# A feed-forward projection by seven block products instead of eight, with streamed weights and outputs summed in SBUF

## The chip, the cores and the metric

The kernel runs on one core of a Trainium2 chip. The metric is the device time of one execution in microseconds. Before the change three runs gave 747.5, 747.75 and 747.91 us, median 747.75. The profiled execution took 747.88 us; its span, from the first to the last recorded work, is 746.0 us.

The core has engines with a queue each: TensorE (PE) multiplies matrices into PSUM, an accumulator memory of eight banks of 128 x 512 floats; VectorE (DVE), ScalarE (ACT) and GpSimd (POOL) work element by element; SyncE (SP) issues the transfers between HBM and SBUF, the on-chip memory.

## The reference

Two branches share an input x of 2048 tokens by 640 features and are mixed by a gate g = sigmoid(x . gate_w):

```python
q, k, v = split(x @ wqkv)                 # 32 heads of 20
phi(a)  = concat(softmax(a @ w_phi), softmax(-(a @ w_phi)))   # per head
a = (phi(q) @ (phi(k)^T v)) / (phi(q) @ sum(phi(k)) + 1e-6) @ wo
h = silu(x @ w1)                          # w1: 640 x 1728
b = h @ w2                                # w2: 1728 x 640
out = g * a + (1 - g) * b
```

All is float32. The change concerns `h` and `b`, called the dense part.

## The kernel before, in words

Everything is computed transposed: features lie on the 128 partitions and tokens along the free axis. 640 features make NC = 5 chunks of 128. The 1728 hidden features make NF = 13 tiles of 128 and a remainder of 64, which counts as tile number 13 (`NF`). The 2048 tokens make NB = 4 blocks of 512.

Float32 accuracy comes from splitting each operand into a high part (rounded to the matmul's input format) and a low part (the difference): `split` (line 124) has ScalarE write the high part and VectorE or GpSimd the low part. A product is then three passes, `PASSES`: high by high, high by low, low by high. For the remainder tile both parts of the weight lie side by side in one stationary operand.

The work has three stages.

1. Keys, values and their state (lines 286 to 706). For 16 token tiles TensorE projects keys and values (`kv_proj`), VectorE and ScalarE make the softmax features (`k_spikes`, `k_sums`), and TensorE sums the state (`kv_acc`). At the end of it the first four hidden tiles of token block 0 are already computed (`h_first`, line 550) as filling, and the state goes to HBM (`kv_out`, then the store to `kv_d` at line 707).
2. The dense part. For each block `dense(b)` (line 936) holds five PSUM banks `acc`, one per output chunk. `h_parts` (line 524) computes one hidden tile in a further bank: 3 passes x 5 chunks = 15 matmuls with 512 tokens each. ScalarE applies silu in place and writes the high part of `u`; VectorE writes the low part. `out_acc` (line 719) then adds that tile's contribution to the five accumulators: 5 x 3 = 15 matmuls. The remainder tile takes 10 and 10. The order of tiles is `ORDERS`; the outputs lag by two tiles. After the last tile `acc_out` multiplies an accumulator by the gate row and stores it to `fb_d` in HBM. All split weights stay in SBUF for the four blocks; `load_f` (line 261) loads and splits them one after the other, nine of them during stage 1 (`NPRE`).
3. In block 3 `last_dense` (line 985) puts other work between the tiles: the fused query weights (`fused`, line 241), the state's layout (`make_kvw`), the split of `wo`, and the query features of the last four token tiles (`q_tile`, `q_rest`). After the dense part (line 1121) the loop `step` does the rest of the queries, the attention's outputs, the product with `wo` and the sum with the rows of `fb_d` (`n_mm`, `w_mm`, `w_add`).

`inorder(...)` fixes an engine's order to the written one. Where it does not name an engine, SyncE above all, a scheduler at build time chooses the order. `raw` gives four buffers for data just loaded; a load waits until the split of the data four loads earlier has been done.

Of the kernel before, what the change touches and what calls it, by code (L numbers as in the profile page):

```python
# [16 lines left out]
P = 128  # L17
# [26 lines left out]
ORDER = (*range(NF - 4), NF, *range(NF - 4, NF))  # L44
END = (0, 4, 5, 6, 7, 8, 9, 1, 2, 3, NF, 10, 11, 12)
ORDERS = (ORDER, ORDER, ORDER, END)
# [16 lines left out]
NEARLY = 3  # L63
PASSES = ((0, 0), (0, 1), (1, 0))
# [3 lines left out]
def mix_kernel(ctx: ExitStack, tc: tile.TileContext, xT, wqT, wkc, wkr, wv, bd, bdc, cst, wo, w1, w1r, w2, out):  # L68
# [61 lines left out]
    PE, DVE, ACT, POOL = E.PE, E.DVE, E.Activation, E.Pool  # L130
# [126 lines left out]
    seq = [(w, f) for f in range(NF) for w in (1, 2)]  # L257
    W = {}
    held = {}

    def load_f(n):
        w, f = seq[n]
        k = n - NPRE
        if 0 <= k < 10:
            if k % 5 == 0:
                held[k // 5] = big(f"f{k // 5}")
            t = held[k // 5][:, k % 5]
        else:
            t = wslot(f"w{w}_{f}", F32R).rearrange("p (s d) -> p s d", s=2) if n < NPRE else fp.tile([P, 2, D], F32R, name=f"w{w}_{f}")
        r = raw(f"wr{w}_{f}")  # L270
        src = w1[f] if w == 1 else w2[f * P : (f + 1) * P, :]
        nc.sync.dma_start(r[:, :D], src)
        split(t[:, 0, :], t[:, 1, :], r[:, :D], "pool" if n < NPRE else "dve")
        W[w, f] = t
# [249 lines left out]
    def h_parts(b, f):  # L524

        ph = bank(f"ph{b}_{f}")
        xt = X["f", b]
        u = slot(f"u{b}_{f}", fu, "u", 3)
        hs = ph
        if f == NF:  # L530
            hs = ur = fu.tile([P, 512], F32, tag="ur", name=f"ur{b}_{f}", bufs=2)
        if f < NF:
            todo = [(W[1, f][:, hw, c * P : (c + 1) * P], xt[c][:, hx, :]) for hw, hx in PASSES for c in range(NC)]
        else:
            todo = [(W1R[:, c, :], xt[c][:, hx, :]) for hx in range(2) for c in range(NC)]
        for n, (lhs, rhs) in enumerate(todo):
            nc.tensor.matmul(ph, lhs, rhs, start=(n == 0), stop=(n == len(todo) - 1))  # L537
        yield u
        if f < NF:
            nc.scalar.activation(hs, ph, AF.Silu)  # L540
            split(u[:, 0, :], u[:, 1, :], hs)
        else:
            nc.scalar.copy(ur[:FR], ph[FR:])
            nc.vector.tensor_tensor(ur[:FR], ph[:FR], ur[:FR], op=ALU.add)
            nc.scalar.activation(ur[:FR], ur[:FR], AF.Silu)
            nc.scalar.copy(u[:FR, 0, :], ur[:FR])
            nc.vector.tensor_tensor(u[FR:, 0, :], ur[:FR], u[:FR, 0, :].bitcast(F32), op=ALU.subtract)
        yield

    def h_first(f, chunks):  # L550

        for c in chunks:
            for hw, hx in PASSES:
                nc.tensor.matmul(  # L554
                    kvp[f % 2],
                    W[1, f][:, hw, c * P : (c + 1) * P],
                    X["f", 0][c][:, hx, :],
                    start=(c == 0 and hw == 0 and hx == 0),
                    stop=(c == NC - 1 and hw == 1),
                )  # L560

    def u_silu(f):
        us0[f] = slot(f"u0_{f}", fu, "u", 3), fu.tile([P, 512], F32, tag="ur", name=f"ur0_{f}", bufs=2)
        last["silu"] = nc.scalar.activation(us0[f][1], kvp[f % 2], AF.Silu)

    def u_hi(f):
        u, ur = us0[f]
        nc.scalar.copy(u[:, 0, :], ur)

    def u_lo(f):  # L570
        u, ur = us0[f]
        nc.vector.tensor_tensor(u[:, 1, :], ur, u[:, 0, :].bitcast(F32), op=ALU.subtract)
        us0[f] = u

    def h_tile(b, f):
        part = h_parts(b, f)
        u = next(part)
        next(part)
        return u
# [23 lines left out]
    us0 = {}  # L603
    phs, eks = {}, {}
    X["f", 0] = []
    xf0 = x_loads("f", 0, X["f", 0])
    with inorder(ACT, DVE, POOL):
# [41 lines left out]
        rw = raw("wr2_3")  # L649
        w23 = wslot("w2_3", F32R).rearrange("p (s d) -> p s d", s=2)  # L650
        nc.sync.dma_start(rw[:, :D], w2[3 * P : 4 * P, :])
        W[2, 3] = w23
        with inorder(PE):
# [4 lines left out]
            kv_rest(t - 2, phs[t - 2])  # L658
            v_part(t, 0, 0)
# [18 lines left out]
            nc.scalar.copy(w23[:, 0, :], rw[:, :D])  # L678
# [10 lines left out]
            nc.gpsimd.tensor_tensor(w23[:, 1, :], rw[:, :D], w23[:, 0, :].bitcast(F32), op=ALU.subtract)  # L689
# [11 lines left out]
            kv_out()  # L701
            u_lo(2)
            nc.vector.tensor_scalar_add(g1, g1, 1.0)
            nc.vector.reciprocal(g, g1)
            nc.vector.tensor_scalar(g1, g, -1.0, 1.0, op0=ALU.mult, op1=ALU.add)
            u_silu(3)
    nc.sync.dma_start(kv_d[: KF + 1], kvo[1])
    u_hi(3)
    u_lo(3)
# [6 lines left out]
    def bank(name):  # L716
        return ps.tile([P, 512], F32, tag="bank", name=name, bufs=8)

    def out_acc(order, f, u, acc, m):
        ds = slice(m * P, (m + 1) * P)  # L720
        if f < NF:
            todo = [(W[2, f][:, hw, ds], u[:, hu, :]) for hw, hu in PASSES]
        else:
            todo = [(W2R[:, k, ds], u[:, 0, :]) for k in range(2)]
        for n, (lhs, rhs) in enumerate(todo):
            nc.tensor.matmul(  # L726
                acc[m], lhs, rhs, start=(f == order[0] and n == 0), stop=(f == order[-1] and n == len(todo) - 1)
            )

    with tc.issue_after(last["silu"].ins):  # L730
        for n in range(NPRE, len(seq)):
            load_f(n)
    r = raw("w1rr")
    W1R = fp.tile([P, NC, P], F32R, name="w1_r")
    rv = r[:, : NC * FR].rearrange("p (c f) -> p c f", f=FR)
    nc.sync.dma_start(r[:, : NC * FR], w1r)
    split(W1R[:, :, :FR], W1R[:, :, FR:], rv)
    r = raw("w2rr")
    W2R = fp.tile([P, 2, D], F32R, name="w2_r")
    for k in range(2):  # L740
        nc.sync.dma_start(r[k * FR : (k + 1) * FR, :D], w2[NF * P :, :])
    nc.scalar.copy(W2R[:, 0, :], r[:, :D])
    nc.vector.memset(W2R[FR:, 1, :].bitcast(F32), 0.0)
    nc.vector.tensor_tensor(W2R[:FR, 1, :], r[:FR, :D], W2R[:FR, 0, :].bitcast(F32), op=ALU.subtract)

    wor_raw = {}
# [5 lines left out]
    def wo_split(c):  # L752
        r = wor_raw.pop(c)
        split(WO[:, c, 0], WO[:, c, 1], r[:, :D])

# [14 lines left out]
    def q_proj(t):  # L770
        if t // 4 == NB - 1:
            parts = [bank(f"pq{t}_{j}")[:, None, :HALF] for j in range(2)]
# [163 lines left out]
    def dense(b):  # L936

        order = ORDERS[b]
        acc = [bank(f"acc{b}_{m}") for m in range(NC)]
        us = {} if b else us0  # L940

        def add(n):
            for m in range(NC):
                out_acc(order, order[n], us[order[n]], acc, m)

        def acc_mm(m):
            for f in order[-3:]:
                out_acc(order, f, us[f], acc, m)

        def acc_out(m):  # L950
            o = fp.tile([P, 512], F32, tag="o", name=f"o{b}_{m}", bufs=3)
            nc.vector.tensor_tensor(o, acc[m], gates[b], op=ALU.mult)
            nc.sync.dma_start(fb_d[m, :, b * 512 : (b + 1) * 512], o)

        return order, us, add, acc_mm, acc_out

    gates = {}

    def load_gates(b):
        if b == 0:  # L960
            pg = bank("pg")
            nc.tensor.transpose(pg[:NT, :P], g1, ident)
            gT = fs.tile([P, 8 * H], F32, tag="sm", name="gT", bufs=3)[:NT, :P]
            nc.scalar.copy(gT, pg[:NT, :P])
            nc.sync.dma_start(g_d, gT)
        gates[b] = fp.tile([P, 512], F32, tag="G1", name=f"G1_{b}", bufs=1)
        nc.sync.dma_start(gates[b], g_d.rearrange("t p -> (t p)")[b * 512 : (b + 1) * 512].partition_broadcast(P))

    for b in range(NB - 1):
        load_x("f", b + 1)  # L970
        order, us, add, acc_mm, acc_out = dense(b)
        for n, f in enumerate(order):
            if f not in us:
                us[f] = h_tile(b, f)
            if n == 4:
                load_gates(b)
            if 1 < n < NF:
                add(n - 2)
        for m in range(NC):
            acc_mm(m)  # L980
            acc_out(m)

    order, us, add, acc_mm, acc_out = dense(NB - 1)
# [405 lines left out]
```

## Time and profile before

| | |
|---|---|
| median of three runs | 747.75 us |
| profiled execution | 747.88 us |
| its span | 746.0 us |
| TensorE busy | 741.4 us, 4177 matmuls |
| VectorE, ScalarE, GpSimd busy | 347.3, 264.1, 255.3 us |
| transfers | 50.30 MB, 67 GB/s over the span |
| dense part on TensorE | 186.9 to 573.2 us |

A row of a group reads: line, engine, operation, output <- input by the program's names, shape, count, then busy time in us, mean duration of one in ns, and the idle time of its engine just before, with what ended it. A row of the timeline reads: start, duration, engine, line, operation. A row of the chain in order of time reads: start, duration, engine, output tile, line, count. The slices cut the span in 40 equal parts of 18.65 us; each digit is the busy share in tenths. PE's weight loads have rows of their own (PEld) and lie beside the matmuls. SPq is SyncE's queue of transfers.

### The profile page before, as it was taken

What the parts mean: (1) busy time and instruction counts of PE and PEld (TensorE: products, weight loads), DVE (VectorE), ACT (ScalarE), POOL (GpSimd) and SP (SyncE); (2) the same over time, 40 slices, a digit from 0 to 9 for tenths busy, and PEclk for the clock granted to TensorE, in tenths of its full rate; (3) what the DMA queues carried; (4) which work ended last, traced back from release to release, by engine and by line L of the source; (5) the groups of instructions that cost most, each with busy time, mean ns of one, the idle gap of its engine ahead of it and who ended that gap; (6) DMA issues with size and microseconds to landing.
All of it is one profiled execution on the core that took longest, in us unless ns stands there. A gap on an engine that the chain in (4) does not pass through costs nothing.

```text
span 746.0 us, 10458 instructions
## 1 busy us (share of the span) xinstructions
PE 741.4 (99%) x4177; PEld 648.0 (87%) x4177; DVE 347.3 (47%) x619; ACT 264.1 (35%) x477; POOL 255.3 (34%) x158
## 2 busy tenths in 40 slices
PE   9999999999999999999999999999999999999998
PEld 8899998888888888888888888888898899999988
DVE  5677666676651220112200122123566776867652
ACT  5444443346542311123111221123553544345230
POOL 2488777767100000000000000000174578686540
PEclk9999999999999999999999999999999999999999
DMA  7111111103650130001300013022102231221222
GB/s 262 53 54 54 54 54 54 60 34 97 199 193 1 50 106 1 1 0 53 107 0 1 0 42 121 36 77 73 39 29 104 74 104 52 86 78 57 72 86 78
DMA packets 35304, 50.30 MB, mean 67 GB/s; under 512 B 3546, under 2 KB 22890, under 8 KB 35255
## 3 DMA queue, kind: packets, MB, share of 16 engines
q1 hardware_dynamic: 35255, 49.63, 20.2%
q8 instruction: 33, 0.54, 0.3%
q14 instruction: 16, 0.13, 0.1%
HBM read 38.51 MB, written 11.11 MB: 67 GB/s over the span
## 4 chain that ended last, share of the span: by engine, by line
PE 99%; DVE 0%; ACT 0%; issue 0%
PE acc L726 25%; PE ph L537 23%; PE kvp L489 16%; PE pa L1182 10%; PE pq L448 10%; PE pn L1140 3%; PE pT L1007 2%; PE kv L459 2%; PE kvp L554 2%; PE kvp L344 1%; PE kvq L344 1%; PE pwk L332 1%; PE pwq L239 1%; PE warm L313 1%; PE kvp L470 0%; PE pkvt L916 0%
## 5 line engine op out<-in xcount | busy, mean ns | idle before, releaser
L127 DVE TENSOR_TENSOR u<-ph,u 128x512 fp32r<-128x512 f32 x48 | 33.2, 692 | 186.5 <-ACT u L125 186.5
L726 PE MATMUL acc<-u,w 128*128 128x512 f32 x480 | 113.6, 390 | 0.0
L909 POOL MEMSET kvw<- 120x40 f32 x1 | 0.1, 131 | 309.8 <-PE ph L537 309.8
L726 PEld LDWEIGHTS acc<-u,w 128*128 128x128 f32 x480 | 89.7, 188 | 18.6
L537 PE MATMUL ph<-xf,w 128*128 128x512 f32 x420 | 99.3, 389 | 0.0
L540 ACT ACTIVATE ph<-ph 128x512 f32<-128x512 f32 x48 | 27.9, 582 | 190.7 <-PE ph L537 190.6
L537 PEld LDWEIGHTS ph<-xf,w 128*128 128x128 f32 x420 | 78.7, 188 | 16.2
L489 PE MATMUL kvp<-wh,xa 128*128 128x480 f32 (+2 forms) x420 | 92.1, 355 | 0.0
L489 PEld LDWEIGHTS kvp<-wh,xa 128*128 128x128 f32 x420 | 71.9, 188 | 8.2
L1182 PE MATMUL pa<-oT,wo 128*128 128x256 f32 x600 | 77.0, 281 | 0.0
L1182 PEld LDWEIGHTS pa<-oT,wo 128*128 128x128 f32 x600 | 73.8, 188 | 0.8 <-DVE oT L1161 0.8
L824 POOL TENSOR_TENSOR ez<-eq,zbc 128x1280 f32<-128x1280 f32 x16 | 47.0, 2937 | 79.9 <-ACT eq L807 55.9
L726 PE MATMUL acc<-u,f 128*128 128x512 f32 x300 | 71.6, 390 | 0.0
L537 PE MATMUL ph<-xf,f 128*128 128x512 f32 x300 | 71.3, 389 | 0.0
L537 PEld LDWEIGHTS ph<-xf,f 128*128 128x128 f32 x300 | 56.3, 188 | 11.7
L726 PEld LDWEIGHTS acc<-u,f 128*128 128x128 f32 x300 | 56.1, 188 | 11.5
L127 POOL TENSOR_TENSOR ph<-ek,ph 128x1280 fp32r<-128x1280 f32 x16 | 47.5, 2966 | 25.8 <-ACT ph L125 24.4
L448 PE MATMUL pq<-wq,xb 128*128 128x320 f32 x360 | 55.9, 312 | 0.0
L448 PEld LDWEIGHTS pq<-wq,xb 128*128 128x128 f32 x360 | 52.9, 188 | 2.0 <-DVE oT L1161 1.6
L489 PE MATMUL kvp<-wl,xa 128*128 128x480 f32 (+2 forms) x210 | 47.2, 354 | 0.0
L807 ACT ACTIVATE eq<-eq 128x1280 f32<-128x1280 f32 x16 | 20.4, 1276 | 66.4 <-DVE eq L439 66.4
L517 POOL TENSOR_TENSOR ek<-ek,st 128x1280 f32<-128x1280 f32 x16 | 37.9, 2369 | 9.2 <-ACT v L304 6.1
(158 smaller groups left out, 1058.6 us busy)
## 6 DMA issues: line engine op xcount, KB each, us to landing
wr<-w SPq DMA_DIRECT2D x26, 320.0 KB, 4.0
xrf<-xT SPq DMA_DIRECT2D x20, 256.0 KB, 3.6
fb_d<-o SPq DMA_DIRECT2D x20, 256.0 KB, 2.4
y<-fb_d SPq DMA_DIRECT2D x16, 256.0 KB, 2.8
out<-y SPq DMA_DIRECT2D x16, 256.0 KB, 2.3
xra<-xT SPq DMA_DIRECT2D x14, 256.0 KB, 3.1
xrb<-xT SPq DMA_DIRECT2D x12, 256.0 KB, 2.7
wvr<-wv SPq DMA_DIRECT2D x5, 327.0 KB, 5.0
```

Of the source, the lines that this page charges most:

```text
L127: eng.tensor_tensor(lo, src, hi.bitcast(F32), op=ALU.subtract)
L344: nc.tensor.matmul(kv_cols(t, lo, hi), x_of(t)[c][:, hx, :], WKV[hw][:, c, w_cols(lo, hi)], start=(opens and hx == 0 and hw == 0), stop=(c ...
L448: nc.tensor.matmul(dst, xt[c][:, hx, :], w[:, c, hw, lo : lo + n], start=first, stop=(hx == 1 and c == NC - 1))
L489: nc.tensor.matmul(kv_cols(t, lo, hi), xt[c][:, hx, :], WKV[hw][:, c, w_cols(lo, hi)], start=(n == 0), stop=(n == 3 * NC - 1), skip_group_ ...
L517: nc.gpsimd.tensor_tensor(groups(e), groups(e), spread(st[:, 1, :]), op=ALU.mult)
L537: nc.tensor.matmul(ph, lhs, rhs, start=(n == 0), stop=(n == len(todo) - 1))
L540: nc.scalar.activation(hs, ph, AF.Silu)
L726: nc.tensor.matmul(acc[m], lhs, rhs, start=(f == order[0] and n == 0), stop=(f == order[-1] and n == len(todo) - 1))
L807: nc.scalar.activation(Q[t]["e"], Q[t]["e"], AF.Exp)
L824: nc.gpsimd.tensor_tensor(ez, Q[t]["e"], zbc, op=ALU.mult)
L1140: nc.tensor.matmul(pns[u, gp][side * CT : side * CT + lhs.shape[-1], a, :], lhs, f[:w, k * 256 : (k + 1) * 256], start=True, stop=True,)
L1182: nc.tensor.matmul(pa[:, a, :], WO[:, c, hw, ds] if c < NG else WOR[:, ds], o[:, ho, c, :] if c < NG else o[:GW, ho, c, :], start=(k == 0) ...
```

## The change

Hidden tiles are taken in pairs (f, g) = (2p, 2p + 1), and token blocks in two halves of two blocks. For four of the five input chunks a pair's 2 x 2 block matrix product (two tiles by two chunk pairs, times two chunk pairs by two blocks) is formed by seven block products instead of eight. They need four sums of weight blocks and four sums of x blocks; the results are combined by additions. The fifth chunk is multiplied directly. Tiles 12, 10, 11 and the remainder (`SINGLE`) of the first half and tile 12 and the remainder (`REG`) of the second are computed as before. So the first half has five pairs, the second six, of which the last (tiles 10 and 11) comes at the end.

- `pair_mm` yields between its eight groups of matmuls. Products that share a term are accumulated on one another in bank `a`, and read in between. `finish` applies silu in SBUF and splits.
- `out_items` gives the second projection for one pair, block and output chunk as a PSUM group of 6 matmuls (11 for four single tiles). VectorE adds it to `acc`, which is now in SBUF; the first group of a half is copied by ScalarE. At the end of a half GpSimd multiplies by the gate.
- PSUM is divided: two banks `a`, two `b`, four `o`.
- `pair_time` runs one pair's products with the previous pair's outputs between them (`PT`, `PTS`: how many after each), and spreads the preparation (`prep`) over the same places.
- `pair_weights` forms the weight sums and all splits of a pair (sums and low parts on GpSimd, high parts on ScalarE) and stores them to HBM (`w_d`), `w2_loads` the same for the second weight (`w2_d`); in the second half `pair_weights_again` and `w2_again` load the finished parts.
- The x sums are formed by `x_sum` and `x_part` into `XT`, for the first half at the start of the dense part, for the second half during pairs 5 and 6 (`half_sums`). The raw x of the first half for this lies in `acc[1]` and in two `w2` buffers.
- Three chunks of x for block 1 are loaded and split already at the end of stage 1 (`x1_hi`, `x1_lo`). The four early tiles are now 12, 10, 11 and the remainder.
- The end of the dense part is a written order of named pieces, `TAIL`. Query projections there use the `a` banks.
- The build reserves a smaller scratch for transfers (`dynamic_dma_scratch_size=1024`).

The core of the diff:

```diff
-NPRE = 9
+SINGLE = (12, 10, 11, NF)
+REG = (12, NF)
+NPAIR = 6
+PRE = ((1, 12), (1, 10), (1, 11), (1, NF), (2, 12), (2, 10), (2, 11), (2, NF), (1, 0))
...
+            xs1.extend(x1_hi(c) for c in range(3))
             h_first(3, (0,))
             kv_rest(t, phs[t], True)
             kv_acc(t, phs[t])
             h_first(3, range(1, NC))
+            x1_lo(xs1[0])
+            x1_lo(xs1[1])
             kv_out()
+            x1_lo(xs1[2], nc.vector)
...
+    def bank(name, tag="b"):
+        return ps.tile([P, 512], F32, tag=tag, name=name, bufs=4 if tag == "o" else 2)
...
+    def x_sum(i, r, eng=nc.gpsimd):
+        n, a, b = {1: (0, 1, 0), 3: (1, 3, 1), 2: (3, 3, 0), 4: (2, 2, 3)}[i]
+        eng.tensor_tensor(r[n], r[a], r[b], op=ALU.subtract)
+
+    def x_part(i, cc, r):
+        t, d = XT[i, cc], r[{1: 0, 3: 1, 2: 3, 4: 2}[i]]
+        nc.scalar.copy(t[:, 0, :], d)
+        nc.vector.tensor_tensor(t[:, 1, :], d, t[:, 0, :].bitcast(F32), op=ALU.subtract)
...
+    def pair_weights(n):
...
+        for dst, a, b, op in (
+            (a22, a21, a22, ALU.add),
+            (a21, a11, a21, ALU.subtract),
+            (a11, a22, a11, ALU.subtract),
+            (a12, a12, a11, ALU.subtract),
+        ):
+            nc.gpsimd.tensor_tensor(dst, a, b, op=op)
+            yield
+        for t, d in ((wb[:, :, 384:], a22), (wc[:, :, :256], a11), (wc[:, :, 256:], a21), (wd, a12)):
+            nc.scalar.copy(t[:, 0, :], d)
+            nc.gpsimd.tensor_tensor(t[:, 1, :], d, t[:, 0, :].bitcast(F32), op=ALU.subtract)
+            yield
+        WP[n][:] = wf, wb, wc, wd
+        if n < NPAIR - 1:
+            for k, t in enumerate(WP[n]):
+                nc.sync.dma_start(w_d[n][k], t.bitcast(F32))
...
+    def w2_loads(*tiles):
+        for f in tiles:
+            r = w_raw(2, f)
+            yield
+            t = w_tile(2, f, fp)
+            w_hi(2, f, t, r)
+            w_lo(2, f, t, r)
+            if f in w2_d and not kept.get(f):
+                nc.sync.dma_start(w2_d[f], t.bitcast(F32))
+                kept[f] = True
+            yield
...
+        def finish(fj, v):
+            u = U[fj] = u_tile(f"u{n}_{fj[0]}_{fj[1]}")
+            nc.scalar.activation(v, v, AF.Silu)
+            nc.scalar.copy(u[:, 0, :], v)
+            nc.vector.tensor_tensor(u[:, 1, :], v, u[:, 0, :].bitcast(F32), op=ALU.subtract)
+
+        a = bank(f"a{n}", "a")
+        mm(a, wf, 0, x0[:2], True, True)
+        yield
+        v1 = v_tile(f"v1_{n}")
+        nc.scalar.copy(v1, a)
+        yield
+        b = bank(f"b{n}")
+        mm(b, wf, 256, x0[2:4], True, False)
+        mm(b, wf, 512, x0[4:], False, True)
+        yield
+        yield
+        mm(a, ws[1], 384, t(1), False, True)
+        yield
+        v5 = v_tile(f"v5_{n}")
+        nc.vector.tensor_tensor(v5, v1, a, op=ALU.subtract)
+        nc.vector.tensor_tensor(v1, v1, b, op=ALU.add)
+        finish((f, 0), v1)
+        yield
+        d = bank(f"d{n}")
+        mm(d, ws[1], 0, t(4), True, False)
+        mm(d, ws[1], 256, x0[4:], False, True)
+        yield
+        yield
+        mm(a, ws[2], 0, t(2), False, True)
+        yield
+        v6 = v_tile(f"v6_{n}")
+        nc.scalar.copy(v6, a)
+        yield
+        c = bank(f"c{n}")
+        mm(c, ws[3], 0, x1[2:4], True, False)
+        mm(c, wf, 512, x1[4:], False, True)
+        yield
+        nc.vector.tensor_tensor(v6, v6, c, op=ALU.add)
+        finish((f, 1), v6)
+        yield
+        mm(a, ws[2], 256, t(3), False, False)
+        yield
+        nc.vector.tensor_tensor(v5, v5, a, op=ALU.add)
+        nc.vector.tensor_tensor(v5, v5, d, op=ALU.add)
+        finish((g, 0), v5)
+        yield
+        mm(a, ws[1], 256, x1[4:], False, True)
+        yield
+        finish((g, 1), a)
+        yield
...
+                for n, (lhs, rhs) in enumerate(todo):
+                    nc.tensor.matmul(o, lhs, rhs, start=(n == 0), stop=(n == len(todo) - 1))
+                yield
+                if start:
+                    nc.scalar.copy(acc[j][m], o)
+                else:
+                    nc.vector.tensor_tensor(acc[j][m], acc[j][m], o, op=ALU.add)
...
+    PT = (1, 1, 1, 1, 1, 1, 3, 1)
+    PTS = {0: (1, 0, 1, 0, 1, 2), NPAIR - 1: (3, 1, 1, 0, 1, 1, 2, 1), 2 * NPAIR - 2: (1, 1, 1, 1, 1, 0, 0, 0)}
...
+        first = pair_mm(0, 0)
+        twice(first)
+        next(first)
+        prep = thunks(pair_weights(0), 12) + prep
+        slots = 7
+        for f in SINGLE[:2]:
+            twice(h_tile(0, 1, f))
+            emit(prep, 0, slots)
+            slots -= 1
+        make_gates()
+        d2 = out_items(0, SINGLE, (0,), start=True)
+        for k in range(NC):
+            twice(d2)
+            emit(prep, 0, slots)
+            slots -= 1
+        for f in SINGLE[2:]:
+            twice(h_tile(0, 1, f))
+            emit(prep, 0, slots)
+            slots -= 1
...
+            if n == NPAIR - 2:
+                prep = merged(prep, half_sums())
+                load_gates(0)
...
+        for name in TAIL.split():
+            ops.pop(name)()
```

More of the change, by code (lines that the diff above doesn't have):

```diff
@@ L714, in mix_kernel @@
     ps = opened("psf", space=PSUM, reuse_waits="tile")
[L716 to L741, printed above, removed]
@@ L934, in mix_kernel @@
     es = {}
[L936 to L955, printed above, removed]
@@ L969, in mix_kernel @@
[L969 to L983, printed above, removed]
-    def last_dense(n, *extra):
-        part = h_parts(NB - 1, order[n])
-        us[order[n]] = next(part)
-        for w in extra:
-            next(w)
-        next(part)
-        if 1 < n < NF:
-            add(n - 2)
-        for w in extra:
-            next(w)
+    gates = {}
```

553 lines of the change are left out of this document (381 added, 172 removed).

## The prediction

> **What bounds the kernel now.** I read the engine totals first, then the slices, then the chain that ended last.
>
> ```profile
> PE 741.4 (99%) x4177; PEld 648.0 (87%) x4177; DVE 347.3 (47%) x619; ACT 264.1 (35%) x477; POOL 255.3 (34%) x158
> PE   9999999999999999999999999999999999999998
> DVE  5677666676651220112200122123566776867652
> POOL 2488777767100000000000000000174578686540
> GB/s 262 53 54 54 54 54 54 60 34 97 199 193 1 50 106 1 1 0 53 107 0 1 0 42 121 36 77 73 39 29 104 74 104 52 86 78 57 72 86 78
> PE 99%; DVE 0%; ACT 0%; issue 0%
> ```
>
> TensorE is busy in every slice and is 99% of the chain. Slices 11 to 28 are the dense part: VectorE has 0 to 2 tenths there and GpSimd nothing. So time goes away only with matmuls, and the other engines have room for what replaces them. The chain in order of time gives the price of a 512-column matmul:
>
> ```profile
> 372.90 3.40 PE ph L537 x15
> 376.31 3.40 PE acc L726 x15
> 410.31 3.40 PE acc L726 x15
> 413.70 2.27 PE ph L537 x10
> ```
>
> 15 matmuls take 3.40 us, 0.2267 us each. A hidden-tile product, one PSUM group of 15, and an output step, five groups of 3, have the same pitch: short groups and bank changes cost nothing. The table by stage (columns: stretch, length, then busy time and count of PE, PEld, DVE, ACT, POOL, then clock, DMA share, GB/s):
>
> ```profile
> 186.90:266.60 79.70, 79.70 (x354) 65.91 (x353) 31.94 (x47) 29.88 (x50) 2.08 (x3) 1.00 0.34 111
> 266.60:359.50 92.90, 92.90 (x411) 76.92 (x411) 16.77 (x25) 19.73 (x34) 0.00 (x0) 1.00 0.10 32
> 515.00:573.20 58.20, 58.20 (x324) 51.48 (x323) 34.49 (x62) 28.18 (x45) 24.79 (x19) 1.00 0.12 44
> 573.20:746.00 172.80, 169.25 (x1349) 158.59 (x1346) 110.95 (x178) 65.38 (x121) 98.87 (x58) 1.00 0.24 79
> ```
>
> One dense block is 205 + 205 matmuls x 0.2267 = 92.9 us, the whole second row: not one stall.
>
> **The sum's first term.** Two feature tiles times two token blocks cost 4 x 15 = 60 matmuls before. After: seven products of two chunks and three passes (42), and the fifth chunk directly for each of the four results (12), so 54. There are 11 pairs (five in the first half, six in the second): 66 matmuls fewer. Tiles outside the pairs and the second projection keep their counts (55 early + 55 + 50 single, 820 output matmuls). 66 x 0.2267 = 15.0 us less on TensorE, if nothing makes it wait.
>
> **A pair in steady state.** The prices of what follows a product:
>
> ```profile
> L952 DVE TENSOR_TENSOR o<-acc,G 128x512 f32<-128x512 f32 x20 | 13.1, 684 | 20.1 <-PE acc L726 16.0 <-DMA fb_d<-o 4.0
> 455.68 0.58 ACT L540 ACTIVATE ph<-ph 128x512 f32<-128x512 f32 x1 [11.74 <-PE ph L537]
> 456.29 0.59 ACT L125 CAST u<-ph 128x512 fp32r<-128x512 f32 x1
> 456.91 0.69 DVE L127 TENSOR_TENSOR u<-ph,u 128x512 fp32r<-128x512 f32 x1 [2.51 <-ACT u L125]
> ```
>
> TensorE needs 54 + 60 matmuls = 25.8 us per pair. VectorE now has 5 combining operations, 4 low parts and 10 additions of outputs into SBUF: 19 x 0.69 = 13.1 us, and at each of 4 results it waits in its queue for ScalarE's silu and copy, 1.2 us: 17.9 us. I laid the queue along the pair: the products stand at 0, 2.7, 6.1, 8.8, 12.2, 15.0, 18.4 and 23.8 us, with output groups of 1.36 us between them. The closest edge is the last one: bank "a" is written again at 23.8, and the addition that reads it waits behind the low part of the second result (product c ends 17.0, +0.2 +0.69 sum +0.6 +0.6 on ScalarE +0.69 = 19.8, one output addition 20.5, then it: 21.2). Slack 2.6 us. The four output banks are freed 2 us or more before reuse, and output groups wait for no u (next pair's first group 27.2, its u at 23.8). I cost steady pairs at nothing; if VectorE were later by more than 2.6 us per pair, all beyond would show. ScalarE has 10 x 0.59 and weight copies of some 4 us: 10 of 25.8.
>
> GpSimd takes the weights. Prices:
>
> ```profile
> L127 POOL TENSOR_TENSOR w<-wr,w 128x640 fp32r<-128x640 f32 x8 | 12.6, 1572 | 4.1 <-ACT w L125 4.1
> L1200 POOL TENSOR_TENSOR y<-pac,y 128x512 f32<-128x512 f32 (+1 forms) x15 | 16.5, 1111 | 0.0
> 560.74 0.74 POOL L127 TENSOR_TENSOR xb<-xrb,xb 128x256 fp32r<-128x256 f32 x1 [1.27 <-ACT xb L125]
> ```
>
> A pair's weights in the first half are 3 x 1.57 (640 columns), about 1.0 (384) and 8 x 0.74 (four sums, four low parts) = 11.6 us of 25.8. In the second half they are read back ready. Transfers: 1.3 MB of raw weights plus 2.1 + 1.3 MB stored per first-half pair, 4.7 MB in 25.8 us = 182 GB/s; 3.4 MB = 132 GB/s later. Slice 1 moved 262 GB/s, so it fits.
>
> **VectorE against GpSimd.** Three of the four low parts now read SBUF twice, where before one input was PSUM. The trace has this at u<-ur:
>
> ```profile
> 178.26 0.69 DVE L572 TENSOR_TENSOR u<-ur,u 128x512 fp32r<-128x512 f32 x1 [0.81 <-ACT u L568]
> 179.47 2.95 POOL L127 TENSOR_TENSOR ph<-ek,ph 128x1280 fp32r<-128x1280 f32 x1 [2.13 <-ACT ph L125]
> 180.57 2.39 DVE L572 TENSOR_TENSOR u<-ur,u 128x512 fp32r<-128x512 f32 x1 [1.62 <-ACT u L568]
> ```
>
> Alone it takes 0.69 us; started during a GpSimd subtraction it lasts until 0.54 us after that one's end. So a low part may cost 0.69 to 0.69 + 1.57 us. I take 0.3 us extra each (GpSimd is busy 11.6 of 25.8, and half of a 0.74 to 1.57 us operation is left on average); at the edge above even 1.57 fits into 2.6 us, so nothing is added for a pair. [...]
>
> **The start.** With 5 early matmuls fewer the dense part begins 1.1 us sooner, at 185.8.
>
> ```profile
> 184.85 4.13 POOL L600 TENSOR_TENSOR kvm<-kvm,cstt 121x240 f32<-121x240 f32 x6 [0.45 <-DVE kvm L595]
> 189.01 0.36 SPq L707 DMA_DIRECT2D kv_d<-kvm  x1
> xrf<-xT SPq DMA_DIRECT2D x20, 256.0 KB, 3.6
> wr<-w SPq DMA_DIRECT2D x26, 320.0 KB, 4.0
> L127 DVE TENSOR_TENSOR xf<-xrf,xf 128x512 fp32r<-128x512 f32 x19 | 14.0, 785 | 16.1 <-ACT xf L125 16.1
> ```
>
> Products a and b, tiles 12 and 10, a transpose (0.3 taken), five output groups of 11, tile 11 and the remainder: 1.36 + 2.04 + 6.80 + 0.3 + 12.5 + 5.67 = 28.6 us, so the first product that needs a sum of x starts at 214.4. Two subtractions for block 1 (1.1 to 1.3 each) are put ahead of the masks on GpSimd, which so end near 191.6. Then come 6.9 us of pair 0's weights and 8 x 1.11 of x sums, 207.4 at the earliest. The raw x for them lies where the key-value part had its tiles, so some of it loads after the kv_d store, from some 194 on: 2.7 MB at 199 to 262 GB/s land at 204 to 208, and the needed sum, copy and low part end near 211. Margin 3 us, on estimates. Before that, chunk 4 of block 1 waits for a raw buffer that GpSimd frees near 186, as I lay its queue out; landed 189.7, split about 191.5, needed 191.9. I take 2 us for the start, between 0 and 5.
>
> **The change of halves** (pairs 5 and 6 in time). VectorE gets 8 more low parts and 2 sums, 10 x 0.785 = 7.9 us, on 17.9: 25.8 of 25.8, with GpSimd at 6 x 1.11 beside it. Eight raw loads (2.1 MB), ready weights (2.1 MB) and stores (1.3 MB) come together. I take 1.5 us, between 0 and 5.
>
> **The end.** Per tile of the last queries:
>
> ```profile
> L432 DVE TENSOR_REDUCE mmq<-pq 128x16 f32<-128x320 f32 x8 | 3.8, 481 | 4.3 <-PE pq L448 4.3
> L811 DVE TENSOR_REDUCE sm<-eq 128x64 f32<-128x1280 f32 x4 | 5.9, 1484 | 4.0 <-ACT eq L807 4.0
> L827 DVE TENSOR_REDUCE sm<-ez 128x64 f32<-128x1280 f32 x3 | 4.4, 1477 | 0.0
> L127 DVE TENSOR_TENSOR wo<-wo,wo 128x640 fp32r<-128x640 f32 x5 | 3.9, 822 | 2.6 <-ACT wo L125 2.6
> 556.41 4.39 PE pq L448 x30
> ```
>
> The written order puts two output groups (5.0 us) behind each query projection (4.39): TensorE 9.4 us per tile. VectorE has 8 x 0.48 + 1.48 + 1.48 + about 0.6 of small ones + 0.82 + 2 x 0.69 = 9.6. Nearly level, and the projections now have two PSUM banks where eight were shared; each is free about 1.5 us before reuse as I lay it out. Four final groups and transposes stand behind the last tile. Put at 0.5 us, from -1 (3.5 us of TensorE's idle time lie after 573.2 today) to 3.
>
> **DMA issues.** The stream adds some 60 transfers of weights and 16 of x, each 0.3 to 0.4 us of SyncE, some 25 us in 370: room enough. But its queue is in order:
>
> ```profile
> SPq L235 <- DVE xf L127: 81.1, 3, 79.6
> SPq L272 <- POOL w L127: 71.8, 7, 16.6
> SPq L272 <- DVE f L127: 6.7, 5, 1.8
> ```
>
> A load behind a store waits for the GpSimd operation the store waits for. Who waits in turn: ScalarE's copy of that weight, and the silus behind it. I cost it at nothing, since a pair's loads are a pair ahead; the second rival is its price if not.
>
> **Sum.** Against the profiled execution, 747.88 (span 746.0, 1.9 around it; the median of the runs is 747.75): 747.9 - 15.0 + 2.0 + 1.5 + 0.5 = **736.9 us**. Its own range is 733 to 741.
>
> **Rivals.** (1) All is covered: 747.9 - 15.0 = 732.9, less at the end perhaps 731.5. For it: the flat 99%. Against it: the three seams. (2) *Slower: SyncE's order.* Stores of the split weights stand ahead of the next loads, so ScalarE waits a load's 4.0 us three times per first-half pair (second w2 tile, two w1 tiles, their stores between). Less the 2.6 us of slack that is 1.4 x 3 = 4.2 us x 5 pairs = 21: 747.9 - 15 + 4 + 21 = 758. It decides from 2.2 us per first-half pair on (11 us in all). For it: the waits above, of up to 79.6 us. Against it: today's queue was mostly ordered so that late ones hurt nobody. (3) *VectorE and GpSimd block each other at the seams.* Some 23 all-SBUF low parts and sums fall at the start and the change of halves, each up to 1.11 longer; with 12 us shown instead of 4, 745. [...] For it: 2.39 against 0.69. Against: the engines' free time around the seams. That the matmuls don't go away can't be; their number is in the code.
>
> **Chances.** Forecast 0.62; all covered 0.08; seams 0.12; no change 0.03; SyncE's order or something like it 0.15. A difference under 0.2% (1.5 us) can't be told from none here. Faster 0.82, same 0.03, slower 0.15. The range 732 to 746 leaves out the slow rival, no change and the tip of the best.
>
> **What would show it.** TensorE's count falls by 66 and its busy time by about 15; VectorE's rises by about 100 us (110 additions, 55 combinations, 16 low parts of x, less 20 gate products and 17 weight parts), GpSimd's about as much; DMA reaches near 89 MB. Steady pairs repeat every 25.8 us; idle time of TensorE stands at about 186 to 216, at the change of halves and in the last 70 us of the dense part. I am wrong if steady pairs are longer than 26.5 us, if ScalarE waits for DMA inside them, or if the seams show more than 9 us.

## The result, and the profile after

The changed kernel takes 743.86 us (four runs, 743.7 to 744.15) against 747.63 for the kernel before beside it: a ratio of 0.995, 95% interval 0.9932 to 0.9967. It gains 3.8 us where 10.9 were forecast. Its profiled execution took 744.15 us, span 742.4.

The page of the changed kernel, the same parts as before (engine totals, slices, transfers, shares of the chain):

```profile
PE 731.1 (98%) x4111; PEld 635.1 (86%) x4111; DVE 440.6 (59%) x750; ACT 302.4 (41%) x561; POOL 381.3 (51%) x271
...
PE   9999999999989999999999999999998999999998
...
DVE  4677666675562355567723544563786776767652
...
POOL 2388777867665632523520004202489678676540
...
DMA packets 47563, 91.38 MB, mean 123 GB/s; under 512 B 4922, under 2 KB 24394, under 8 KB 47511
...
PE 86%; DVE 4%; POOL 3%; DMA 2%; ACT 2%; issue 1%; SPq 0%; POOLq 0%; ACTq 0%; DVEq 0%
```

The work moved as the code says: 66 matmuls fewer, VectorE 93 us and GpSimd 126 us more, 91.4 MB instead of 50.3. TensorE still fills the slices, but two of them (12 and 31) are down to 8 tenths, and 14% of the chain now lies off TensorE. The same three stretches by stage, before and then after (columns as in the prediction's table by stage):

```profile
184.00:245.00 61.00, 61.00 (x272) 50.41 (x271) 27.31 (x43) 25.69 (x45) 4.53 (x7) 1.00 0.39 124
245.00:495.00 250.00, 250.00 (x1115) 207.37 (x1114) 48.70 (x74) 52.89 (x93) 0.00 (x0) 1.00 0.13 42
495.00:592.00 97.00, 96.67 (x565) 84.90 (x565) 53.31 (x89) 43.00 (x74) 34.76 (x28) 1.00 0.19 64
```

```profile
184.00:245.00 61.00, 57.75 (x241) 45.37 (x240) 29.16 (x38) 33.28 (x67) 37.76 (x38) 0.97 0.55 184
245.00:495.00 250.00, 249.95 (x1102) 206.37 (x1101) 129.78 (x194) 89.04 (x159) 75.37 (x68) 1.00 0.51 181
495.00:592.00 97.00, 93.98 (x573) 81.41 (x571) 67.30 (x112) 41.20 (x79) 55.39 (x42) 1.00 0.27 91
```

In the middle stretch, which holds the steady pairs and the change of halves, next to nothing is missing: 249.95 of 250 us busy. In the first, 241 matmuls went through where 272 did, and the clock is 0.97. In the last, 3.0 us of idle time stand where 0.3 did. Taking every matmul's start and adding up by how much each step exceeds the usual one, I find 6.9 us lost in the first stretch (before: 0.1), 0.3 in the second (0), 5.6 in the third (1.7). That is 11.1 us more than before, and -15.0 + 11.1 = -3.9, against -3.7 between the two profiled executions: the whole result. The gain is there; two seams gave most of it back. The longest waits of TensorE name them:

```profile
PE pT L1352 <- ACT fT L1368: 2.0, 1, 2.0
PE o L968 <- DVE u L587: 1.9, 1, 1.9
...
PE ph L594 <- DVE xf L651: 0.5, 1, 0.5
...
PE pT L1352 <- POOL eq L1102: 0.4, 1, 0.4
```

**The start.** The timeline of the changed kernel:

```profile
187.21 3.36 POOL L673 TENSOR_TENSOR kvm<-kvm,cstt 121x240 f32<-121x240 f32 x5
...
187.86 3.26 DVE L651 TENSOR_TENSOR xo<-xr,xo 128x512 fp32r<-128x512 f32 x1 [0.46 <-ACT xo L646]
...
191.94 0.74 PE L594 MATMUL ph<-xf,w 128*128 128x512 f32 x2 [0.48 <-DVE xf L651]
...
217.22 0.62 ACT L804 CAST xo<-xr 128x512 fp32r<-128x512 f32 x1 [0.56 <-POOL xr L800]
...
217.75 0.58 ACT L598 ACTIVATE ph<-ph 128x512 f32<-128x512 f32 x1
...
221.62 0.69 DVE L587 TENSOR_TENSOR u<-ur,u 64x512 fp32r<-64x512 f32 x1 [1.35 <-ACT u L586]
...
222.36 0.79 PE L968 MATMUL o<-u,w 128*128 128x512 f32 x2 [1.90 <-DVE u L587]
```

A low part of block 1 on VectorE lasts 3.26 us, through five of GpSimd's masks in a row, where one alone takes 0.69; TensorE waits 0.5 us for the next one. Then the x sums are slow. Rows of the lines that form a sum (L800, GpSimd) and its low part (L805, VectorE), durations in ns as minimum/median/maximum (a start after 300 us belongs to the change of halves):

```profile
L800 POOL TENSOR_TENSOR acc<-acc,acc x4: 1288/1296/1617, 204.7 to 209.1; 128x512 f32<-128x512 f32 x4
L800 POOL TENSOR_TENSOR xr<-xr x4: 1305/1685/1751, 210.3 to 339.7; 128x512 f32<-128x512 f32 x4
L805 DVE TENSOR_TENSOR xo<-acc,xo x4: 1215/1504/1775, 206.7 to 212.6; 128x512 fp32r<-128x512 f32 x4
```

The prediction had 1.11 and 0.785 us. Its 1.11 was a mean over two shapes; the shape of the sums alone takes 1.30 in the kernel before:

```profile
L1200 POOL TENSOR_TENSOR y<-pac,y 128x512 f32<-128x512 f32 x10 | 13.0, 1298 | 0.0
```

So blocking added up to 0.45 us to a sum, and 0.5 to 1.1 us to most low parts. The sums also began late, at 204.66 us: ahead of them on GpSimd stand the low parts of pair 0's weights, whose high parts ScalarE copies behind two silus. One wait for such a copy is

```profile
POOL wb L833 <- ACT wb L832: 4.1, 1, 4.1
```

and another lasts 1.4 us. But the product on the first sums is not what waits. ScalarE makes the high parts of the sums (L804), in order, each waiting for its sum; behind them stand the silus of tile 11 and of the remainder. Tile 11's product was complete at about 213.9, its silu (L598) starts at 217.75, the remainder's low part (L587) ends at 222.3, and only then can block 1's first output group go on. And a second thing follows (windows of 1 us; the third last column is the clock):

```profile
222.00:223.00 1.00, 0.64 (x3) 0.53 (x4) 0.97 (x2) 0.00 (x0) 0.00 (x0) 0.94 0.00 0
223.00:224.00 1.00, 1.00 (x4) 0.81 (x3) 0.71 (x2) 0.22 (x1) 0.00 (x0) 0.50 0.00 0
...
226.00:227.00 1.00, 1.00 (x5) 0.83 (x4) 0.00 (x0) 0.93 (x2) 1.00 (x1) 0.85 0.00 0
```

Right after the wait TensorE is granted half its clock for 0.12 + 3 + 0.30 = 3.4 us: the eight matmuls in it start 0.427 us apart, 1.6 us lost. The last section has the waits behind which half clock came in the other kernels, and those behind which it did not.

**The end.** Timeline of the changed kernel, the third group of four transposes (L1352) of the query features:

```profile
560.55 1.27 ACT L1049 ACTIVATE eq<-eq 128x1280 f32<-128x1280 f32 x1 [7.46 <-DVE eq L480]
...
561.73 0.57 ACT L1368 COPY fT<-pT 120x512 f32<-120x512 f32 x1
...
562.35 0.65 PE L1352 MATMUL pT<-ident,eq 128*120 128x128 f32 x4 [2.02 <-ACT fT L1368]
```

The transposes use the two `b` banks in turn. The copy that frees one stands on ScalarE behind an exp, and that exp behind VectorE's subtraction: TensorE waits 2.0 us.

### The profile page after: what moved, and what is told of

Its sections match the earlier page's. It is cut to its first block, busy times and chain, and to the rows that moved or that the text cites. A ratio compares the mean times of both kernels' runs of the same rounds, so it can differ in the third digit from the quotient of the medians.

```text
span 742.4 us, 10812 instructions
## 1 busy us (share of the span) xinstructions
PE 731.1 (98%) x4111; PEld 635.1 (86%) x4111; DVE 440.6 (59%) x750; ACT 302.4 (41%) x561; POOL 381.3 (51%) x271
## 4 chain that ended last, share of the span: by engine, by line
PE 86%; DVE 4%; POOL 3%; DMA 2%; ACT 2%; issue 1%; SPq 0%; POOLq 0%; ACTq 0%; DVEq 0%
PE o L968 20%; PE kvp L530 16%; PE pa L1501 10%; PE a L896 8%; PE pq L489 7%; PE d L896 3%; PE c L896 3%; PE pn L1459 3%; PE b L896 3%; PE kv L500 2%; PE pT L1352 2%; PE ph L594 2%; PE kvp L613 1%; PE kvp L385 1%; PE kvq L385 1%
## 5 line engine op out<-in xcount | busy, mean ns | idle before, releaser
L968 PE MATMUL o<-u,w 128*128 128x512 f32 x820 | 203.4, 391 | 2.3 <-DVE u L587 1.9
L968 PEld LDWEIGHTS o<-u,w 128*128 128x128 f32 x820 | 152.9, 188 | 35.5 <-DVE u L587 2.3
L305 POOL TENSOR_TENSOR w<-wr,w 128x640 fp32r<-128x640 f32 x26 | 41.1, 1596 | 184.9 <-ACT w L294 184.9
L973 DVE TENSOR_TENSOR acc<-acc,o 128x512 f32<-128x512 f32 x100 | 66.8, 683 | 53.0 <-PE o L968 53.0
L905 ACT ACTIVATE v<-v 128x512 f32<-128x512 f32 x33 | 20.9, 632 | 116.0 <-DVE v L924 57.1
L907 DVE TENSOR_TENSOR u<-v,u 128x512 fp32r<-128x512 f32 x33 | 24.6, 746 | 42.6 <-ACT u L906 42.6
L530 PEld LDWEIGHTS kvp<-wl,xa 128*128 128x128 f32 x210 | 36.6, 188 | 4.5
L1102 POOL TENSOR_TENSOR eq<-eq,sm 128x1280 f32<-128x1280 f32 x16 | 37.9, 2366 | 1.0 <-DVE sm L1096 0.8
L984 POOL TENSOR_TENSOR acc<-acc,G 128x512 f32<-128x512 f32 x20 | 27.4, 1387 | 20.6 <-DVE acc L973 20.6
L138 POOL TENSOR_TENSOR xa<-xra,xa 128x512 fp32r<-128x512 f32 (+1 forms) x26 | 26.5, 1046 | 17.4 <-ACT xa L136 17.4
```

What stands on the lines that cost most here:

```text
L138: eng.tensor_tensor(lo, src, hi.bitcast(F32), op=ALU.subtract)
L305: eng.tensor_tensor(t[:, 1, :], r[:, :D], t[:, 0, :].bitcast(F32), op=ALU.subtract)
L530: nc.tensor.matmul(kv_cols(t, lo, hi), xt[c][:, hx, :], WKV[hw][:, c, w_cols(lo, hi)], start=(n == 0), stop=(n == 3 * NC - 1), skip_group_ ...
L968: nc.tensor.matmul(o, lhs, rhs, start=(n == 0), stop=(n == len(todo) - 1))
L973: nc.vector.tensor_tensor(acc[j][m], acc[j][m], o, op=ALU.add)
L984: nc.gpsimd.tensor_tensor(acc[j][m], acc[j][m], gates[j], op=ALU.mult)
```

## The experiments

The kernel before took 747.79 to 747.92 us beside them; ratios are to it.

**Tiles first.** All four single tiles of block 1 ahead of the outputs, so that their silus stand ahead of the x sums.

```diff
-        for f in SINGLE[:2]:
+        for f in SINGLE:
...
-        for f in SINGLE[2:]:
-            twice(h_tile(0, 1, f))
-            emit(prep, 0, slots)
-            slots -= 1
```

> Tile 11 and the remainder of block 1 are multiplied ahead of block 0's outputs. Theory A (order on ScalarE): in the changed kernel their silus stand behind copies of x sums, TensorE waits 3.1 us for them at 218.5 to 222.4 us and then runs 3.41 us at half clock, 1.6 us more. With the silus early, both go: 743.9 - 4.7 = 739.2. Theory B (VectorE and GpSimd block each other, the x sums are late): the wait only moves to the first product with an x sum, at 216 us; then no more than 2 us come back, 742 or above.

741.22 us (740.3 to 741.31), ratio 0.991 [0.9895, 0.9925]. The wait for L587 and the half clock behind it are gone from the profile; the start loses 2.9 us instead of 6.9. ScalarE's order is thus a cause, though the gain is less than expected. The start gave back 4.0 us of the 4.7 counted on, and the clock differs: in the profiled run the clock was 1.000 throughout and that execution took 740.3; in the three others it was 0.998, and they took 741.2 to 741.3.

**Sums on VectorE.**

```diff
-            prep += [(0, lambda i=i, cc=cc: x_sum(i, raws[cc])) for i in (1, 3, 2, 4)]
+            prep += [(0, lambda i=i, cc=cc: x_sum(i, raws[cc], nc.vector)) for i in (1, 3, 2, 4)]
```

> The eight x sums at the start move from GpSimd to VectorE, order as it was. Theory B: a sum takes 0.69 us instead of 1.29 to 1.74, the low parts 0.69 instead of 1.2 to 1.8, since GpSimd reads nothing beside them; the copies end some 4 us sooner and with them the silus behind: 739 to 740. Theory A expects the same gain from another cause, as the order is harmful only while the sums are late. If VectorE's own 16 operations in a row (11 us) are now the late ones, no gain: 744.

741.73 us (741.42 to 742.03), ratio 0.992 [0.9905, 0.9935]. The same low parts, in this kernel's instructions of L805:

```profile
L805 DVE TENSOR_TENSOR xo<-acc,xo x4: 686/686/687, 207.4 to 209.2; 128x512 fp32r<-128x512 f32 x4
```

0.69 instead of 1.2 to 1.8 us: with the sums off GpSimd, nothing blocks them. The start loses 2.7 us. That the total is some 2 us above the expectation is for the most part the clock again: after the 2.0 us wait for the transposes, which in the changed kernel cost only itself, this kernel has 3.4 us at half clock (mean clock 0.56 from 559 to 561 us and 0.58 from 561 to 563).

**Two more banks for the transposes.** The last two of the four groups of transposes go into the `a` banks.

```diff
-            ops[f"tm{i}"] = lambda i=i: t_mm(0, i, bank)
+            ops[f"tm{i}"] = lambda i=i: t_mm(0, i, lambda name: bank(name, "ab"[i < 2]))
```

> Two of the four groups of transposes at the end take the banks of the query projections. If TensorE's 2.0 us wait at 560 us (the copy out of the bank stands behind the last exponential on ScalarE) is lost time: 743.9 - 2.0 = 741.9. Rival: the last query tile's features, which end with GpSimd's product at 577.1, are due next; then the wait at 576.4 grows from 0.6 to 2.6 us and the time stays at 743.5 to 743.9.

745.35 us (744.03 to 746.34), ratio 0.9967 [0.9954, 0.998]. Its longest wait:

```profile
PE pT L1352 <- POOL eq L1102: 2.7, 1, 2.7
```

The bank wait is gone, TensorE comes earlier to the last tile's product on GpSimd, and now waits 2.7 us for that; in the changed kernel this row read 0.4. The expectation's rival had this wait, at 2.6 us. The profiled run's clock is 0.995, against 0.997 in the changed kernel, and the kernel is 1.5 us slower than the change.

**One product less.** A product is left out of every pair, to see whether TensorE sets the pace inside the pairs.

```diff
-        mm(d, ws[1], 0, t(4), True, False)
-        mm(d, ws[1], 256, x0[4:], False, True)
+        mm(d, ws[1], 256, x0[4:], True, True)
```

> One of the seven block products is left out of every pair (the two-chunk part of d, 6 matmuls in each of 11 pairs), so the third result of a pair is incomplete; all the rest is unchanged. If TensorE bounds every pair and VectorE's queue has the slack of my layout (17.9 us of 25.8): 66 x 0.2267 = 15.0 us less, 729. If VectorE, ScalarE or GpSimd is close behind, pairs stay longer than 24.5 us and less than 10 us come back.

731.82 us (731.37 to 731.97), ratio 0.9786 [0.9769, 0.9802]: 12.0 us less than the change for 66 matmuls fewer, 15.0 us of work. So pairs are TensorE's, and the covering engines have room even with 24.5 us per pair; the change of halves then begins to show (1.0 us waiting for VectorE's L923), and the waits for L1367's copies grow from one of 2.0 to two of 3.1 in all.

**Filler at the wait.** Twelve matmuls whose result nobody reads, ahead of block 1's first output group.

```diff
+    def fill(name, n):
+        o = bank(name, "o")
+        for i in range(n):
+            nc.tensor.matmul(o, W[1, 0][:, 0, :P], X["f", 0][0][:, 0, :], start=(i == 0), stop=(i == n - 1))
...
+            if counts is PTS[0] and k == 0:
+                fill("fill", 12)
```

> Twelve matmuls that nobody reads (2.7 us) stand ahead of block 1's first output, where TensorE waited 3.1 us in the changed kernel; order and data of the rest are as they were, so the wait for the silus still ends at 222.4 us. If the 3.41 us at half clock that followed came from the few matmuls before it, it goes away: 743.9 - 1.6 = 742.3, granted clock 1.0. If the half clock comes from something else at this place (transfers, the time), it stays: 743.9 or up to 2 more.

743.63 us (742.63 to 744.82), ratio 0.9947 [0.9932, 0.9962]. TensorE's wait for L587 is down to 0.6 us. But the runs fall apart: clock 1.000 with 742.63 and 743.16, so no half clock at the start, and clock 0.998 with 744.09 and 744.82, 1.6 us more. In the profiled one (744.82) the only wait above 1.1 us is the 2.0 us one for the transposes; I put its half clock there. So the runs of one kernel differ by 1.6 us as they have such a stretch or not.

**Another order at the end**, with the two more banks: in `TAIL`, GpSimd's two products of the last tile (`qn15`, `qm15`) stand ahead of gates and outputs that came before them.

```diff
-qe15 tm0 qs15 ia6 qm14 ig5 to0 xs1 im7 qc15 tm1 tm2 xs2 qn15 ia7 qN15 im8 ia8 to2 tm3 ig6 qP15 im9
-ig7 ia9 qi15 qw15 ig8 to3 to1 ig9 qm15
+qe15 tm0 qs15 ia6 qm14 qn15 to0 xs1 im7 qc15 tm1 tm2 xs2 ig5 ia7 qN15 im8 ia8 to2 tm3 ig6 qP15 im9
+ig7 ia9 qi15 qw15 qm15 ig8 to3 to1 ig9
```

> The two more banks of before, and on GpSimd the last tile's two products come ahead of the gates and x parts that stood before them (4 us and 2.5 us of other work moved behind). If that product's end at 577 us is what the end of the dense part waits for, it comes at least 2.5 us sooner, and the waits of 2.0 and 0.6 us on TensorE both go: 743.9 - 2.6 = 741.3. If VectorE's queue of the last tile is the cause, the wait stays with it and the time at 743 to 744.

747.63 us (ten runs, 745.79 to 749.61), ratio 1.0 [0.999, 1.001]: a miss. The wait has moved a second time. Its timeline:

```profile
566.88 9.20 SPq L986 DMA_DIRECT2D fb_d<-acc  x5
...
577.20 1.92 SPq L1495 DMA_DIRECT2D y<-fb_d  x4
...
579.16 5.36 SPq L227 DMA_DIRECT2D xrb<-xT  x5
...
582.73 0.41 ACT L136 CAST xb<-xrb 128x256 fp32r<-128x256 f32 x1 [3.74 <-DMA xrb<-xT]
583.04 2.53 ACT L1368 COPY fT<-pT 120x512 f32<-120x512 f32 x5
...
583.67 1.53 PE L1352 MATMUL pT<-ident,eq 128*120 128x128 f32 x6 [3.31 <-ACT fT L1368]
```

SyncE issues the stores of the dense part's output as GpSimd finishes them, behind them the loads `y` that read them back, and behind those the last x for the queries. ScalarE waits 3.74 us for that x, the copies that free the banks stand behind its cast, and TensorE waits 3.3 us. After it the clock is at half for 6.8 us in the profiled run (clock 0.995); runs at 0.997 and 0.993 took 745.8 and 747.9 to 749.6. Its start is the changed kernel's, with the same 1.9 us wait for L587, but in this execution no half clock followed that wait: the 6.8 us account for its clock of 0.995.

**All three**: tiles first, sums on VectorE, and the order at the end with its two banks.

> Tiles first, x sums on VectorE and the new end together. Sum of the parts: start 4.0 less waiting and 1.6 less at half clock (4.7 by the traces of the two start edits together), end 2.6: 743.9 - 4.7 - 2.6 = 736.6. If the phases hide each other's waits, 738 to 740.

743.22 us (743.0 to 744.43), ratio 0.9944 [0.9929, 0.9959]: a miss by the same wait, here 3.2 us; the profiled run's clock is 0.998, and no other wait of TensorE is above 1.1 us.

**Block 1's x on GpSimd, ahead of the masks**, added to that.

```diff
-            x1_lo(xs1[0])
-            x1_lo(xs1[1])
-            kv_out()
-            x1_lo(xs1[2], nc.vector)
+            for c in range(3):
+                x1_lo(xs1[c])
+            masks = kv_out()
+            for c in range(3, NC):
+                x1_lo(x1_hi(c))
+            for b, mask in masks:
+                nc.gpsimd.tensor_tensor(b, b, mask, op=ALU.mult)
...
-        for c in range(3, NC):
-            x1_lo(x1_hi(c), nc.vector)
```

> The kernel with all three, and the low parts of block 1's x stand on GpSimd ahead of the key-value masks, where two stood on VectorE beside them; the sum that frees a PSUM bank is taken first. By blocking, one low part lasted 3.26 us and TensorE waited 0.5 + 1.1 us at 187 to 194: those go, 736.6 - 1.5 = 735.1. If GpSimd's queue is now late with the masks and what loads behind them, the wait comes back at the first x sum: 736.6 or more.

741.27 us (740.22 to 742.16), ratio 0.9914 [0.99, 0.9929]. The start now loses 0.3 us in all. The 2.9 us wait at the end is what remains.

**The start alone**: tiles first, sums on VectorE, block 1's x on GpSimd; the end as in the change.

> The three edits at the start (tiles first, x sums on VectorE, block 1's low parts on GpSimd ahead of the masks), the end as in the changed kernel. If the losses at the start are independent of the end: 6.9 - 0.3 = 6.6 us less than the changed kernel, 737.3. If what is won at the start only makes the end wait longer (as at the end, where each edit moved the wait on), 740 or above.

739.92 us (739.67 to 740.16), ratio 0.9895 [0.9878, 0.9911]: 3.9 us off the change. Most of the excess over the expectation lies in two places: 0.6 us waiting for the first x sum, and 3.4 us of half clock right after the 2.0 us wait for the transposes (windows of 2 us):

```profile
555.00:557.00 2.00, 0.41 (x4) 0.41 (x5) 0.90 (x1) 2.00 (x3) 2.00 (x2) 1.00 0.00 0
557.00:559.00 2.00, 2.00 (x9) 1.64 (x8) 1.78 (x3) 1.31 (x5) 2.00 (x3) 0.69 0.34 131
559.00:561.00 2.00, 2.00 (x6) 1.53 (x5) 0.00 (x0) 0.00 (x0) 2.00 (x2) 0.50 0.38 131
```

**The last x ahead of the loads of y**, added to the kernel of the eighth experiment.

```diff
+        with tc.issue_after(last["xb"].ins):
             nc.sync.dma_start(y[:, :n], fb_d[m0 : m0 + n, :, cols].rearrange("m p s -> p m s"))
...
-            x_ahead(p)
+            last["xb"] = x_ahead(p)
```

> All edits of the start and of the end, and in addition the next loads of x are put ahead of the loads of y in SyncE's queue. If the 3 us wait on transposes at 575 to 578 us is the x load's place in that queue (behind y loads, which wait for the last gated stores): the load issues 2.5 us sooner and 741.3 becomes 738.8. If it is held by the stores alone, no gain: 741.

**736.25 us** (735.68 to 736.86), ratio 0.9845 [0.983, 0.9859], the fastest of all. Its three longest waits of TensorE:

```profile
PE warm L354 <- DVE ones L177: 1.1, 1, 1.1
PE kvp L385 <- ACT wh L136: 0.8, 2, 0.5
PE ph L594 <- ACT kvw L1169: 0.5, 1, 0.5
```

The first two stand ahead of the dense part; neither seam has a long wait any more. It beat its expectation, in which half clock was left in, while all four of its runs have a clock of 1.000. Even so it lies 3.4 us above the 732.9 of the first rival, in which all is covered.

**The end alone**: order, banks and the pinned loads, with the start as in the change.

> The three edits of the end (two more banks, GpSimd's order, x loads ahead of y loads), the start as in the changed kernel. The kernel with only the first two of them took 747.6 us, with a 3.3 us wait on transposes. If that wait was SyncE's order, it is gone and the end loses 3.4 instead of 5.6 us beside its half-clock windows: 743.9 - 2.2 = 741.7, and up to 1.6 less where the end had a half-clock window; the gains of start and end add up: 739.9 + 741 - 743.9 = about 736.3 to 738 for both. If the order of the queue matters only with an earlier start, 745 or more.

742.03 us (740.83 to 742.94), ratio 0.9915 [0.9899, 0.9932], as expected. Against the same order without the pin it is 5.6 us less: that is what SyncE's order alone cost there, the half clock behind its wait included. Its queue:

```profile
568.66 9.19 SPq L986 DMA_DIRECT2D fb_d<-acc  x5
577.94 0.89 SPq L227 DMA_DIRECT2D xrb<-xT  x2
579.00 1.88 SPq L1496 DMA_DIRECT2D y<-fb_d  x4
```

Start alone -3.9, end alone -1.8, both -7.6: more than their sum. With one seam still waiting for 2 us, half clock followed there: in the profiled run with the start alone at the end (clock 0.50 from 559 to 561 us), in the one with the end alone at the start (0.97 from 184 to 245 us). With both quiet there was none (1.000 in all four runs).

## Why the prediction was right and wrong

*Right: the main term and its cover.* TensorE has 66 matmuls fewer, and steady pairs run at 25.84 us, as the chain in order of time shows by the first product of each pair:

```profile
242.43 1.36 PE a L896 x6
...
268.27 1.36 PE a L896 x6
```

TensorE had no wait in them, so the slack at bank `a` was never used up, and leaving a product out shortened the pairs: the 15.0 us are real. The change of halves, put at 1.5, lost 0.2 to 0.4 us. TensorE's part of the final tiles came at 9.4 us per tile as forecast, the projections at 521.59, 531.00, 540.40 and 549.81.

*Right inside the pairs, wrong as a whole: SyncE's order costed at nothing.* A sign of being wrong was that ScalarE waits for transfers inside the pairs. ScalarE's waits for transfers between 242 and 345 us, the steady pairs of the first half, are

```profile
ACT wb L832 <- DMA wr<-w: 0.7, 1, 0.7
ACT w L294 <- DMA wr<-w: 0.4, 1, 0.4
```

and hurt nobody; the slower rival fails there. In the changed kernel the order is close behind at the end as well: the chain that ended last passes through a load of x from 578.02 to 582.13 us, though TensorE loses some 0.2 us there. Its mechanism, a load behind a store that waits for GpSimd, is what the end turned into as soon as its nearer waits were taken away.

*Wrong: "I take 2 us for the start".* It lost 6.9: 1.7 ahead of 194 us (a bank and block 1's x), 3.0 from 218 to 222 us waiting for the silus' results, 1.6 at half clock, the rest in small steps. Four things failed. First, the sums and their low parts were mis-sized, 1.3 to 1.75 and for the most part 1.2 to 1.8 us instead of 1.11 and 0.785: 1.11 was a misread mean, and the engines block each other (a low part took 0.69 us once the sums were on VectorE as well). I charged that price, 2.39 against 0.69 us in the kernel before, to the pairs, where it is hidden, but in the sum not to the x sums, where it isn't. Second, "6.9 us of pair 0's weights" behind masks that end near 191.6 put the first sum at 198.5; it started at 204.66, since GpSimd waited for ScalarE's copies. The last sum ended at 217.2, where the prediction had 207.4 at the earliest. (It also read slices 11 to 28 as holding 0 to 2 tenths of VectorE; slices 11 and 12, where the start lies, already had 6 and 5.) Third, the step "the needed sum, copy and low part end near 211. Margin 3 us" followed only the product that reads the sums; that product did run without a wait. I did not name what is queued behind the waiting copies on ScalarE, the silus of tile 11 and of the remainder. Last, a wait's price was taken as its length: 1.6 us of half clock came on top. Both single edits cut the loss to less than half (2.9 and 2.7 of 6.9), so slow sums and ScalarE's order are two links of one chain; how much each has of the first wait can't be parted further.

*Wrong: "Put at 0.5 us" for the end.* It lost 3.9 more than before, 2.0 of it in the wait at the transposes. The step that failed is "Nearly level". VectorE's 9.6 us per tile were its work alone, and TensorE's are 9.4; but the exps, each of which follows VectorE's subtractions of its tile, came every 10.9 us, from the first to the third:

```profile
527.90 1.27 ACT L1049 ACTIVATE eq<-eq 128x1280 f32<-128x1280 f32 x1 [2.99 <-DVE eq L480]
...
549.79 1.27 ACT L1049 ACTIVATE eq<-eq 128x1280 f32<-128x1280 f32 x1 [6.34 <-DVE eq L480]
```

Between the second and the third, VectorE stood still for 2.3 of 10.9 us, 1.4 waiting for the exp itself and 0.9 for GpSimd. So the first exp starts 6.3 us after its projection did and the last one 10.7, and behind that one stands the copy that frees the transposes' bank. The chain that ended last runs through these engines, not TensorE, from 526 us to that copy; no run speeds them up, so this link is read from the trace and not tested. The prediction's "free about 1.5 us before reuse" speaks of the projections' banks, for which TensorE never waited; for the two `b` banks of the transposes it had no term at all. The experiments show three waits in line at one place, each hidden by the one before: banks, GpSimd's last product, SyncE's loads.

With what was lost in place of what was put, the sum gives 747.9 - 15.0 + 6.9 + 0.3 + 3.9 = 744.0. The prediction's own sign, more than 9 us at the seams, came true with 11.1. The total is near the 745 that the third rival gives, but not by its mechanism alone: blocking is part of the start's loss and none that I could find of the end's.

## What to carry to other kernels

In a kernel at 99% of one engine, what a change takes off that engine is worth what its seams leave of it; follow the in-order queues of the helpers there (ScalarE's and SyncE's, not only the two engines that block each other), and ask of every late instruction what stands behind it. Removing the wait that shows is not enough at such a seam, since the next one comes up: at the end of the dense part the first edit, and the first two, lost time, and the three together gained 1.8 us. The 1.9 us wait at the start cost 3.5, 1.6 of them at half clock, so look at the granted clock behind each wait.

## What the runs showed of the hardware

Half clock came in stretches of 3.4 us, and not after each wait of 1.9 us or more. It came behind the 1.9 us wait at the start in the changed kernel, from 222.89 to 226.30 us (clock 0.50); behind the 2.0 us at the transposes with the sums on VectorE and with the start alone, 3.4 us each; and behind 3.3 us with the other order at the end, 6.8 us. It did not come behind the 2.0 us at the transposes in the changed kernel (clock 1.00 in each window of 2 us from 556 to 566 us) and with the tiles first (1.000 over the whole profiled execution), nor behind the 1.9 us at the start with the other order at the end. What decides was not shown. One stretch is worth 1.6 us: runs of the kernel with the filler lie that far apart (742.6 to 743.2 against 744.1 to 744.8). The gains at the two seams do not add, 3.9 and 1.8 us alone and 7.6 together; for the executions without a profile only the mean clock is known.

VectorE's subtraction of 128 x 512 takes 0.69 us alone and lasted longer beside GpSimd's work: 2.39 us beside one GpSimd subtraction in the kernel before, 1.2 to 1.8 beside GpSimd's x sums in the changed kernel, against 0.69 with those sums away, and 3.26 through five short masks in a row.
